# A chunked recurrence with a phase mixer on one core: each on-chip transpose either whole into one PSUM bank or as pairs of 64-row blocks into two, all eight banks in one tile, and a new table of the order

## The chip, the core and the metric

The kernel runs on one core of one Trainium2 chip. A core has a matrix engine (PE, with its weight loads shown apart as PEld), a vector engine (DVE), a scalar engine (ACT), GpSimd (POOL) and a queue engine (SP) that issues most DMAs. They run side by side and wait for each other through semaphores. PE writes to PSUM alone, which has eight banks; ACT and DVE copy from there to SBUF, and POOL works on SBUF.

The metric is the device time in microseconds. Before the change it is 198.57 us, the median of three runs (198.26 to 198.94). All inputs and the output are float32; the tolerance leaves room for bf16 matmuls, which both kernels use.

## What is computed

Two stages, the second on the output of the first. B = 4 batches, H = 8 heads, S = 768 tokens, D = 40.

```
state = zeros(B, H, D, D)
for t in range(S):
    y[:, :, t] = einsum('bhd,bhde->bhe', rt, state)
    Sa = einsum('bhde,bhe->bhd', state, at)
    state = state * wt[:, :, None, :] - einsum('bhd,bhe->bhde', Sa, bt)
    state = state + einsum('bhd,bhe->bhde', vt, kt)

x = y.transpose(0, 2, 1, 3).reshape(B, S, H * D)        # 4 x 768 x 320
theta = x @ w_theta
zr, zi = x * cos(theta), x * sin(theta)
u = x + einsum('ts,bsd->btd', w_tok_r, zr) + einsum('ts,bsd->btd', w_tok_i, zi)
out = u + maximum(u @ w_ch, 0)
```

## The kernel before

**Tiles.** The 768 tokens of a batch are cut into six chunks of 128; the 24 pairs of batch and chunk are the tiles i = 0 to 23, and a batch is six tiles in a row. In a tile the recurrence over 128 tokens becomes triangular products between matrices, two heads (64 padded rows each) side by side in a group of 128; there are four groups.

**Work of one tile**, by the names that the prediction uses:

- SP loads six arrays of 160 KB: w, k, b, a, v and r (`loads`; L409, and L421 for r and the first eight v).
- ACT takes the logarithm of w; PE makes its running sums (`cs`, L461); ACT makes the exponentials `ex` and `we`.
- POOL multiplies k and b by `ex` (`kb`, L429) and a by `we` (`ah`, L429).
- PE transposes these operands by matmuls against an identity: `tkb` (eight blocks of 128 by 128), `ta` (four), for tiles 8 and on `tv` (four), all at L391; for r and the first eight v `tr` and `to` (eight blocks for two tiles, L538) and `tb` (four, L557). ACT (L394) or DVE (L397) copies the result from PSUM to SBUF (`ekb`, `ea`, `ev`, `er`, `eb`).
- PE makes four score matrices: `spsi`, `sphi`, `slv`, `slu`, each by eight matmuls of 64 rows (L569). The two heads of a group use the upper and the lower 64 rows of the array, and write to two different banks. Each matrix of 128 by 1024 is masked on its way out by DVE (L578), or copied by ACT (L580) and masked by a select on POOL (L582).
- The chain from tile to tile: `x0` (L610, L616), copy `nx`, `nu` (L629), copy `enu`, then the new state `gt` (L652, L663, L667) and its copy for the readout `gd`; `nu` is transposed as well (`nut`, four blocks, L391).
- Readout: `y` (L793 to L802), times `we` on DVE, gives x.

**Work of the mixer.** For each two tiles, x is transposed (`xt`, five blocks, L711) and multiplied by w_theta (`th`, L763, L773). For each batch ACT makes sines and cosines, POOL the products `z` (L865), and for each of six output rows PE adds up twelve matmuls of 128 by 320 (`row`, L881). DVE adds x; then `ut` (five blocks, L711), `ch` (L763, L773), the last DVE operation and the store. The tokens' weights are transposed once (`wt`, six blocks each, L968).

**What sets the order.** Nothing is scheduled at run time or by a compiler: the code records 1602 operations (`Plan.add`), each with what it reads and writes, and then emits them in the order of the table `ORDER`. An engine runs its own operations in that order and waits at each for what it needs. `PICK` lists operations that run on their second engine instead of the first (a copy on DVE instead of ACT, for example). `HOMES` gives each PSUM result its bank. `WARM` puts matmuls on a constant in front of some early operations.

**PSUM before.** There are two tiles of two banks (`ps_d`) and four tiles of one bank (`ps_s`). The scores, which need two banks, go to the first; all else, transposes included, goes to the second, one bank each. A transpose of n blocks is n matmuls in the array's full 128-row mode.

## Time and profile before

The profile is one execution by the hardware profiler. Its own time is the span from its first to its last instruction.

| what | value |
|---|---|
| time, median of 3 runs | 198.57 us (198.26 to 198.94) |
| span of the profiled execution | 197.811 us |
| granted TensorE clock, mean | 1.000 |
| POOL: busy us, share | 145.1, 73% |
| moved by DMA | 32.75 MB, mean 166 GB/s |
| instructions of PE (matmuls) and PEld (weight loads) | 3288 each |

How to read it: a busy time is the union of an engine's instructions. Matmuls are pipelined, each is shown with its whole latency (some 0.2 to 0.3 us), and the next starts long before the one ahead has ended; so how dense PE runs is read from the distance between starts, in the timeline, and not from the busy time. A row of the timeline has the start in us, the length from the first start to the last end, the engine, the line, the operation, its shape, and the number of instructions that were merged. A row of the groups has the count after x, then the busy us and the mean ns of one, then the idle time ahead of them. The shape 64*128 means that 64 of the array's 128 rows are used.

### The profile page before, as it was taken

To read this page: it belongs to the slowest core of one execution; us is meant where nothing else is said; L and a number is where in the kernel's file an instruction comes from. 1 tells how busy PE (TensorE), PEld (TensorE's weight loads), DVE (VectorE), ACT (ScalarE), POOL (GpSimd) and SP (SyncE) were. 2 spreads that over 40 slices of the span, in tenths; PEclk is the share of its full clock that TensorE was granted. 3 is DMA by queue.
4 is the path that set the end of the run, shared out by engine and by line. 5 is a ranking of instruction groups with operands and counts; after the bars stand their busy time and mean duration, and the time that the engine had idled before them with its cause. 6 is when DMAs were issued, how large, how long until landed. Compare 5 with 4: busy or idle time off the path is not lost.

```text
span 197.8 us, 8019 instructions
## 1 busy us (share of the span) xinstructions
PE 187.6 (95%) x3288; PEld 150.3 (76%) x3288; DVE 164.3 (83%) x261; ACT 151.7 (77%) x337; POOL 145.1 (73%) x210
## 2 busy tenths in 40 slices
PE   7888999999989999999999999999999999999992
PEld 6776787777768788878878888888887878767661
DVE  5269899999989999888887988999999988675453
ACT  3584979799889988979988598888998986575111
POOL 8267544679879999699799939769699697558100
PEclk9999999999999999999999999999999999999999
DMA  6999879989999999999998899988998274863055
GB/s 119 210 212 163 154 161 196 182 166 197 233 174 173 207 171 185 190 185 223 153 210 168 153 187 170 188 148 169 182 155 163 43 177 102 87 194 104 0 191 174
DMA packets 134644, 32.75 MB, mean 166 GB/s; under 512 B 124816, under 2 KB 134608, under 8 KB 134608
## 3 DMA queue, kind: packets, MB, share of 16 engines
q1 hardware_dynamic: 131680, 29.19, 75.1%
q0 software_dynamic: 2784, 2.97, 9.6%
q8 instruction: 25, 0.41, 0.9%
q10 hardware_dynamic: 144, 0.08, 0.1%
q14 instruction: 11, 0.09, 0.1%
HBM read 29.54 MB, written 3.93 MB: 169 GB/s over the span
## 4 chain that ended last, share of the span: by engine, by line
PE 68%; DMA 9%; ACT 8%; SPq 6%; DVE 3%; issue 3%; POOL 1%; ACTq 0%; DVEq 0%; POOLq 0%
PE ps_s L881 17%; PE ps_s L391 10%; PE ps_d L569 9%; PE ps_s L763 5%; SPq L409 4%; DMA raw_w<-in_w_dram 3%; DMA raw_kb<-in_k_dram 3%; PE ps_s L711 3%; PE ps_s L652 2%; PE ps_s L629 2%; SPq L421 2%; DMA raw_r<-in_r_dram 2%; PE ps_s L538 2%; PE ps_s L773 2%; ACT cs L850 2%
## 5 line engine op out<-in xcount | busy, mean ns | idle before, releaser
L429 POOL TENSOR_TENSOR kb<-raw_kb,ex 128x320 bf16<-128x320 f32 x46 | 36.8, 811 | 9.7 <-DMA raw_kb<-in_k_dram 3.3
L881 PE MATMUL ps_s<-zr,wtok_r 128*128 128x320 bf16 x132 | 37.6, 299 | 0.0
L881 PE MATMUL ps_s<-zi,wtok_i 128*128 128x320 bf16 x132 | 37.5, 299 | 0.0
L578 DVE TENSOR_TENSOR lamu<-ps_d,mask_p 128x1024 bf16<-128x1024 f32 x22 | 26.8, 1219 | 1.7 <-PE ps_d L569 1.6
L578 DVE TENSOR_TENSOR psi<-ps_d,mask_p 128x1024 bf16<-128x1024 f32 x22 | 26.8, 1218 | 1.6 <-PE ps_d L569 1.4
L578 DVE TENSOR_TENSOR lamv<-ps_d,mask_p 128x1024 bf16<-128x1024 f32 x17 | 20.7, 1218 | 2.6 <-PE ps_d L569 1.8
L429 POOL TENSOR_TENSOR ah<-raw_a,we 128x320 bf16<-128x320 f32 x22 | 19.0, 866 | 3.6 <-DMA raw_a<-in_a_dram 1.6
L578 DVE TENSOR_TENSOR phi<-ps_d,mask_n 128x1024 bf16<-128x1024 f32 x17 | 20.7, 1218 | 0.9 <-PE ps_d L569 0.8
L865 POOL TENSOR_TENSOR zi<-cs,xp 128x320 bf16<-128x320 f32 x21 | 16.9, 816 | 3.3 <-ACT cs L850 3.3
L881 PEld LDWEIGHTS <-wtok_r 128*128 128x128 bf16 x144 | 14.0, 97 | 4.5
L569 PE MATMUL ps_d<-aT,kbT 64*128 64x128 bf16 x384 | 17.1, 217 | 0.2
L881 PEld LDWEIGHTS <-wtok_i 128*128 128x128 bf16 x144 | 14.1, 98 | 3.5
L391 PE MATMUL ps_s<-wide,kb 128*128 128x128 bf16 x184 | 15.0, 223 | 1.0 <-POOL kb L429 0.7
L865 POOL TENSOR_TENSOR zr<-cs,xp 128x320 bf16<-128x320 f32 x19 | 15.3, 810 | 0.7 <-ACT cs L850 0.7
L667 POOL TENSOR_TENSOR gt<-sum,ex 128x320 bf16<-128x320 f32 x13 | 9.5, 733 | 8.0 <-DVE sum L663 4.8
L800 PE MATMUL ps_s<-kb,lamv 128*128 128x40 bf16 x192 | 15.0, 180 | 0.0
L802 PE MATMUL ps_s<-kb,lamu 128*128 128x40 bf16 x192 | 14.9, 179 | 0.0
L569 PEld LDWEIGHTS <-kbT 64*128 64x128 bf16 x384 | 11.8, 94 | 3.1 <-ACT kbT L394 1.0
L800 PEld LDWEIGHTS <-lamv 128*128 128x128 bf16 x192 | 13.2, 96 | 0.6
L887 DVE TENSOR_TENSOR up<-ps_s,xp 128x320 bf16<-128x320 f32 x22 | 10.7, 488 | 3.5 <-PE ps_s L881 3.1
L435 POOL CAST r<-raw_r 128x640 bf16<-128x640 f32 x12 | 8.6, 720 | 6.5 <-DMA raw_r<-in_r_dram 6.5
L445 ACT ACTIVATE lw<-raw_w 128x320 bf16<-128x320 f32 x24 | 11.4, 475 | 2.6 <-DMA raw_w<-in_w_dram 2.6
(176 smaller groups left out, 606.7 us busy)
## 6 DMA issues: line engine op xcount, KB each, us to landing
raw_w<-in_w_dram SPq DMA_DIRECT2D x24, 160.0 KB, 4.1
raw_v<-in_v_dram SPq DMA_DIRECT2D x24, 160.0 KB, 3.9
raw_a<-in_a_dram SPq DMA_DIRECT2D x24, 160.0 KB, 4.2
raw_kb<-in_k_dram SPq DMA_DIRECT2D x24, 160.0 KB, 3.7
raw_kb<-in_b_dram SPq DMA_DIRECT2D x24, 160.0 KB, 4.0
raw_r<-in_r_dram SPq DMA_DIRECT2D x24, 160.0 KB, 4.4
out_dram<-oo SPq DMA_DIRECT2D x9, 160.0 KB, 2.0
wrow_i<-in_moe_w_tok_i_dram POOLq DMA_DIRECT2D x6, 192.0 KB, 5.3
```

Source lines behind the costliest of these rows:

```text
L391: nc.tensor.transpose(out=dst[:, c:c + 128], in_=pair(src, g), identity=ident)
L429: pool = ("POOL", lambda: nc.gpsimd.tensor_tensor(out=dst, in0=in0, in1=in1, op=ALU.mult))
L445: add("ACT", "ln", i, lambda: nc.scalar.activation(out=paired(lw)[:, :, :, 0:D], in_=paired(raw_w[s4]), func=AF.Ln), 473, [("raw_w", s4)], ...
L569: nc.tensor.matmul(t[:, q, g, :], lhsT=lhs[g][rows(q)], rhs=rhs[g][rows(q)], start=True, stop=True)
L578: add("DVE", kindm, i, lambda: nc.vector.tensor_tensor(out=flat, in0=whole(), in1=mask.to_broadcast([128, 2 * G, 128]), op=ALU.mult), 1217 ...
L667: add("POOL", "wgt", i, lambda: nc.gpsimd.tensor_tensor(out=new_state, in0=sum_t, in1=wm.to_broadcast([128, 8, D]), op=ALU.mult), 830, [(" ...
L763: nc.tensor.matmul(ps(pk)[:, 0:DM], lhsT=lhs[:, 3 * c + kt, :], rhs=wt[:, 3 * c + kt, :], start=kt == 0, stop=kt == 2, skip_group_check=n ...
L800: nc.tensor.matmul(o, lhsT=lamv[:, p, g, :], rhs=kb[:, 0, h, 0:D], start=first, stop=False, skip_group_check=True)
L802: nc.tensor.matmul(o, lhsT=lamu[:, p, g, :], rhs=kb[:, 1, h, 0:D], start=False, stop=True, skip_group_check=True)
L865: pool = ("POOL", lambda: nc.gpsimd.tensor_tensor(out=dst, in0=in0, in1=in1, op=ALU.mult))
L881: nc.tensor.matmul(acc(), lhsT=wtok[nm][j][:, s], rhs=zs[c][:, s], start=n == 0 and c == 0, stop=n == NT - 1 and c == 1)
L887: add("DVE", "uadd", q, lambda: nc.vector.tensor_tensor(out=u, in0=acc(), in1=x, op=ALU.add), 488, [pk, x_key(q)], [u_key(q)], at="row")
```

## The change

It has four parts.

1. The eight banks are one tile, `banks`; a result of two banks may lie in any two neighbouring ones.
2. A transpose may be whole as before (`new=(key, 1)`), or split: each block of 128 by 128 becomes two matmuls of 64 rows against a 64 by 64 identity, of which the one writes the first half of the result's columns to one bank and the other the second half to the next (`turned`, and `go` in `turn_runs`). The copy out of PSUM (`evac`) then reads both banks in one instruction, with one more level in its access pattern.
3. `PICK` now also says which transposes are split: 46 operations with 252 blocks in all: 72 of `tkb`, 40 each of `nut` and `tr`, 23 of `ut`, 18 of `wt`, 16 each of `ta` and `tb`, 11 of `xt`, 8 each of `tv` and `to`. Some operations change their engine: ACT goes from 327 to 310, DVE from 236 to 252, POOL from 185 to 189.
4. `ORDER`, `HOMES` and the place of the warm-up matmuls are new.

The diff, with the tables cut to a row each:

```diff
 ORDER = [
-    0, 7, 3, 6, 1, 2, 20, 8, 21, 23, 24, 4, 27, 9, 32, 30, 5, 22, 31, 33, 12, 25, 26, 34, 11,
...
-PICK = [
-    25, 31, 37, 39, 40, 48, 49, 75, 80, 85, 86, 115, 118, 130, 172, 180, 193, 203, 204, 222,
...
-WARM = {21: 25, 30: 4, 33: 1, 28: 8, 41: 11}
+PICK = {
+    26: 1, 32: 1, 36: 1, 38: 1, 40: 1, 41: 1, 48: 1, 49: 1, 75: 1, 77: 1, 78: 1, 85: 1, 86: 1,
...
+WARM = {21: (1, 25), 30: (0, 4), 33: (2, 1), 28: (6, 8), 41: (6, 11)}
...
-        for n in PICK:
-            self.ops[n].eng, self.ops[n].fn = self.ops[n].alts[0]
+        for n, m in PICK.items():
+            o = self.ops[n]
+            o.eng, o.fn = o.alts[m - 1][:2]
+            if o.eng == "PE":
+                o.new = (o.new[0], 2)
...
-    doubles = [psum.tile([128, 2, 512], FP32, name=f"ps_d{i}") for i in range(DOUBLE // 2)]
-    singles = [psum.tile([128, 512], FP32, name=f"ps_s{i}") for i in range(BANKS - DOUBLE)]
+    banks = psum.tile([128, BANKS, 512], FP32, name="banks")
...
-        return doubles[h[0] // 2] if len(h) == 2 else singles[h[0] - DOUBLE]
+        return banks[:, h[0]:h[0] + 2] if len(h) == 2 else banks[:, h[0]]
...
-    def transpose_pairs(dst, srcs):
-        for j, src in enumerate(srcs):
-            for g in range(G):
-                c = (j * G + g) * 128
-                nc.tensor.transpose(out=dst[:, c:c + 128], in_=pair(src, g), identity=ident)
...
-        act = ("ACT", lambda: copy_words(dst, ps(psk)[:, at]))
-        dve = ("DVE", lambda: copy_halves(dst, ps(psk)[:, at]))
+    def turned(kind, i, key, srcs, reads, cost, at="tile"):
+
+        def go():
+            if not split(key):
+                t = ps(key).bitcast(BF16)
+                for m, src in enumerate(srcs()):
+                    nc.tensor.transpose(out=t[:, m * 128:m * 128 + 128], in_=src, identity=ident)
+                return
+            for m, src in enumerate(srcs()):
+                for c in range(2):
+                    nc.tensor.transpose(out=ps(key)[:, c].bitcast(BF16)[:, m * 64:m * 64 + 64],
+                                        in_=src[rows(c)], identity=ident[rows(c), rows(c)])
...
+    def evac(eng, kind, i, psk, dst, n, writes=(), part=None):
+
+        def copy(op, out, dt, w):
+            one, src = n * w // 64, ps(psk) if w == 32 else ps(psk).bitcast(BF16)
+            if not split(psk):
+                at = (part or 0) * one
+                op(out=out, in_=src[:, at:at + one])
+            elif part is not None:
+                op(out=out, in_=src[:, part, 0:one])
+            else:
+                op(out=out.rearrange("p (n c w) -> p c n w", c=2, w=w),
+                   in_=src[:, :, 0:one // 2].rearrange("p c (n w) -> p c n w", w=w))
...
+            def words(x=x, dst=dst):
+                out = dst.bitcast(FP32)
+                if split(pr):
+                    nc.scalar.copy(out=out, in_=ps(pr)[:, x, 0:256])
+                    return
...
-                nc.tensor.matmul(t[:, 0:128], lhsT=busy[:, 0:128], rhs=busy[:, 0:128],
+            at, n = WARM[o.idx]
+            for _ in range(n):
+                nc.tensor.matmul(banks[:, at, 0:128], lhsT=busy[:, 0:128], rhs=busy[:, 0:128],
```

Three places show how the table moves instructions. In the rows, `banks` is the new tile for PSUM, and the number behind a name is the buffer's.

PE in tile 14, between `x0` and `nu`; `up_219` is a pair of mixer rows that `ut` transposes, `vT_195` and `kbT_188` are the weights of the scores `slv` and `sphi`. Before:

```order
L616 LDWEIGHTS psi_198
L616 MATMUL ps_s_253<-v_134,psi_198 128x40
L711 LDWEIGHTS up_219
L711 MATMUL ps_s_254<-wide,up_219 128x128
...
L569 LDWEIGHTS vT_195
L569 MATMUL ps_d_251<-rT_191,vT_195 128x128
```

The same place after the change:

```order
L606 LDWEIGHTS kbT_188
L606 MATMUL banks<-aT_185,kbT_188 128x128
L411 LDWEIGHTS up_219
L411 MATMUL banks<-wide,up_219 128x64
...
L666 LDWEIGHTS phi_200
L666 MATMUL banks<-nx_206,phi_200 128x40
```

The transpose of `up` has gone from the full mode ahead of the scores to ten matmuls of 64 rows and 64 columns behind them, in the mode that the scores have already set.

SP at the start of the program: the loads in the order of their issue. Before:

```order
L409 DMA raw_w_64<-in_w_dram 128x8x40
L421 DMA raw_v_77<-in_v_dram 128x1x320
L409 DMA raw_a_68<-in_a_dram 128x8x40
L421 DMA raw_v_77<-in_v_dram 128x1x320
L409 DMA raw_kb_73<-in_k_dram 128x8x40
L409 DMA raw_kb_73<-in_b_dram 128x8x40
L409 DMA raw_w_65<-in_w_dram 128x8x40
```

After:

```order
L439 DMA raw_w_64<-in_w_dram 128x8x40
L439 DMA raw_w_66<-in_w_dram 128x8x40
L439 DMA raw_w_65<-in_w_dram 128x8x40
L451 DMA raw_v_77<-in_v_dram 128x1x320
L439 DMA raw_kb_73<-in_k_dram 128x8x40
L451 DMA raw_v_77<-in_v_dram 128x1x320
L439 DMA raw_kb_73<-in_b_dram 128x8x40
L439 DMA raw_a_68<-in_a_dram 128x8x40
```

The w of tiles 1 and 2 is now loaded ahead of the other arrays of tile 0, whose last one, a, goes from the third place to the eighth.

POOL between the products of tile 4 (`kb_128`) and those of tile 5 (`kb_129`); AFFINE_SELECT is the mask of a score matrix that ACT has copied. Before:

```order
L429 TENSOR_TENSOR kb_128<-raw_kb_73,ex_174 128x8x40 x2
L435 CAST r_136<-raw_r_80 128x16x40
L429 TENSOR_TENSOR ah_127<-raw_a_68,we_179 128x8x40
L582 AFFINE_SELECT lamv_203<-lamv_203 128x1024
L429 TENSOR_TENSOR kb_129<-raw_kb_74,ex_175 128x8x40 x2
```

After:

```order
L459 TENSOR_TENSOR kb_128<-raw_kb_73,ex_174 128x8x40
L459 TENSOR_TENSOR ah_126<-raw_a_72,we_178 128x8x40
L619 AFFINE_SELECT lamv_203<-lamv_203 128x1024
L619 AFFINE_SELECT phi_201<-phi_201 128x1024
L465 CAST r_136<-raw_r_80 128x16x40
L459 TENSOR_TENSOR kb_129<-raw_kb_74,ex_175 128x8x40
L459 TENSOR_TENSOR ah_127<-raw_a_68,we_179 128x8x40
L992 DMA wrow_i_249<-in_moe_w_tok_i_dram 128x768
L619 AFFINE_SELECT psi_198<-psi_198 128x1024
L619 AFFINE_SELECT lamu_205<-lamu_205 128x1024
L459 TENSOR_TENSOR kb_129<-raw_kb_74,ex_175 128x8x40
```

Where one select stood there are four.

80 lines of the change are left out of this document (32 added, 48 removed), and 238 rows, old and new, of tables (HOMES, ORDER, PICK).

## The prediction

> **What bounds the kernel now.** I read three stretches of the windows first, then the chain of waits, then the timeline. In the rows of the windows the columns are the stretch, its length, then busy us (and instructions) of PE, PEld, DVE, ACT and POOL, then the granted clock, the DMA share and GB/s.
>
> ```profile
> span 197.8 us, 8019 instructions
> 0.00:60.00 60.00, 54.13 (x993) 44.14 (x993) 49.43 (x85) 46.29 (x112) 40.72 (x72) 1.00 0.94 181
> 60.00:160.00 100.00, 99.46 (x1871) 81.80 (x1870) 91.53 (x134) 88.71 (x195) 87.23 (x121) 1.00 0.94 171
> 160.00:197.80 37.80, 34.03 (x431) 24.39 (x428) 23.32 (x44) 16.68 (x32) 17.13 (x20) 1.00 0.50 127
> 57.00:80.00 23.00, 23.00 (x449) 18.96 (x445) 22.29 (x30) 21.64 (x53) 22.55 (x34) 1.00 1.09 185
> 80.00:120.00 40.00, 39.77 (x698) 32.24 (x696) 33.89 (x53) 34.17 (x74) 33.92 (x46) 1.00 0.97 181
> ```
>
> From 60 us on PE is never without work (99.46 of 100 us), while DVE (91.53), ACT and POOL have 8 to 13 us each to spare. Ahead of 60 us every engine has gaps. The chain of waits says why:
>
> ```profile
> 13.29 5.87 DMA raw_kb<-in_k_dram
> 30.21 4.23 DMA raw_r<-in_r_dram
> 48.11 6.82 DMA raw_w<-in_w_dram
> 55.73 0.44 PE ps_s L711 x5
> ```
>
> Three times the chain stands on a load (columns: start, us, what), the last until 54.9 us; behind that it is mostly PE. So the first 55 us are paced by loads that come at 181 GB/s, 0.9 us for 160 KB, and what PE saves there is worth little. What PE saves later is worth its full price, as long as DVE, at 91.5%, can follow.
>
> Now PE itself, from the distance between starts. Whole transposes and scores, at 83 us:
>
> ```profile
> 83.20 0.40 PE L569 MATMUL ps_d<-aT,kbT 64*128 64x128 bf16 x8
> 83.43 0.39 PE L569 MATMUL ps_d<-rT,nuT 64*128 64x128 bf16 x8
> 83.76 0.62 PE L391 MATMUL ps_s<-wide,kb 128*128 128x128 bf16 x8
> 84.22 0.30 PE L881 MATMUL ps_s<-zr,wtok_r 128*128 128x320 bf16 x1
> ```
>
> Eight whole blocks take 84.22 - 83.76 = 0.46 us, 0.056 a block (the rows are rounded to 0.01). Eight score matmuls of 64 rows take 83.43 - 83.20 = 0.23: four pairs at 0.056, so the two of a pair run side by side, and a pair costs what one whole matmul of 128 columns costs. The second eight end their issue at 83.43 + 0.23 = 83.66, and the transpose starts at 83.76: **a change of mode costs 0.10**. Once more:
>
> ```profile
> 108.60 0.71 PE L763 MATMUL ps_s<-wch,uT 128*128 128x320 bf16 x4
> 109.23 0.31 PE L773 MATMUL ps_s<-wch,uT 64*128 64x320 bf16 x2
> 109.38 0.61 PE L569 MATMUL ps_d<-aT,kbT 64*128 64x128 bf16 x16
> 109.92 0.31 PE L881 MATMUL ps_s<-zr,wtok_r 128*128 128x320 bf16 x1
> 110.07 0.30 PE L881 MATMUL ps_s<-zi,wtok_i 128*128 128x320 bf16 x1
> 110.21 0.30 PE L881 MATMUL ps_s<-zr,wtok_r 128*128 128x320 bf16 x1
> ```
>
> One whole matmul of 320 columns costs 0.14 (110.07 to 110.21); the pair of 320 costs 0.15 (109.23 to 109.38). Four whole ones from 108.60 end at 109.14, and the mode changes until 109.23: 0.09. Eight pairs from 109.38 end at 109.83, next start 109.92: 0.09 again. I take 0.095.
>
> **The split blocks.** A split block is a pair of 64 columns, which the trace does not show. Small matmuls do:
>
> ```profile
> 110.92 0.18 PE L800 MATMUL ps_s<-kb,lamv 128*128 128x40 bf16 x1
> 110.95 0.18 PE L802 MATMUL ps_s<-kb,lamu 128*128 128x40 bf16 x1
> 110.97 0.18 PE L800 MATMUL ps_s<-kb,lamv 128*128 128x40 bf16 x1
> 111.00 0.18 PE L802 MATMUL ps_s<-kb,lamu 128*128 128x40 bf16 x1
> ```
>
> Forty columns cost 0.025. Low end: the pair costs no more than that, 0.025. High end: each of its two matmuls costs it, 0.050. By columns, between 0.025 (40) and 0.056 (128), one matmul of 64 is about 0.030. I take 0.031, since both pairs above cost what one matmul of their columns costs. Saved: 0.056 - 0.031 = 0.025 a block (0.006 to 0.031). The change splits 252 blocks; of the operations that they belong to, 99 blocks ran before 60 us and 153 later. Later: 153 x 0.025 = **3.8 us** (0.9 to 4.7). Earlier: 2.5, taken as nothing.
>
> A rule speaks against this. The Trainium skill, TensorE: Matmul & The Clock Gate, Part 1, holds that the distance from start to start never falls below about 25 ns, however few the columns. By it a pair is 50 ns and the 153 blocks save 0.9; the pair in the first fence, at 56 ns for two, would fit either reading.
>
> **The changes of mode.** PE changes between full and 64-row mode 134 times before and 100 times after, as the order has it. By the time at which the operations ran before: 49 become 21 ahead of 60 us, 15 become 7 from 60 to 80, and 70 stay 70 behind (two more fall among the warm-up matmuls). At 0.095 that is 0.8 us from 60 us on, and 2.7 ahead of it, where the loads pace. The place in tile 14 shows the common case late in the program:
>
> ```profile
> 114.05 0.45 PE L711 MATMUL ps_s<-wide,up 128*128 128x128 bf16 x5
> 114.43 0.41 PE L569 MATMUL ps_d<-rT,vT 64*128 64x128 bf16 x8
> ```
>
> Five blocks (0.28) and a change of mode (0.10) before the scores; after the change the blocks follow the scores at 0.16, and the change of mode comes behind them instead.
>
> **The copies.** Masks, small copies and products change their engine. The prices:
>
> ```profile
> L578 DVE TENSOR_TENSOR psi<-ps_d,mask_p 128x1024 bf16<-128x1024 f32 x22 | 26.8, 1218 | 1.6 <-PE ps_d L569 1.4
> L397 DVE COPY kbT<-ps_s 128x1024 bf16<-128x1024 bf16 x8 | 5.5, 686 | 0.3 <-PE ps_s L391 0.2
> L397 DVE COPY aT<-ps_s 128x512 bf16<-128x512 bf16 x8 | 3.4, 420 | 0.8 <-PE ps_s L391 0.7
> L623 DVE CAST nx<-ps_s 128x320 bf16<-128x320 f32 x2 | 1.0, 486 | 0.2 <-PE ps_s L616 0.2
> L582 POOL TENSOR_SCALAR_AFFINE_SELECT phi<-phi 128x1024 bf16<-128x1024 bf16 x7 | 7.6, 1093 | 1.0 <-ACT phi L580 1.0
> L429 POOL TENSOR_TENSOR ah<-raw_a,we 128x320 bf16<-128x320 f32 x22 | 19.0, 866 | 3.6 <-DMA raw_a<-in_a_dram 1.6
> L435 POOL CAST r<-raw_r 128x640 bf16<-128x640 f32 x12 | 8.6, 720 | 6.5 <-DMA raw_r<-in_r_dram 6.5
> L865 POOL TENSOR_TENSOR zi<-cs,xp 128x320 bf16<-128x320 f32 x21 | 16.9, 816 | 3.3 <-ACT cs L850 3.3
> L546 ACT COPY rT<-ps_s 128x256 f32<-128x256 f32 x24 | 8.2, 378 | 1.6 <-DVE sx L482 0.8 <-PE ps_s L538 0.7
> L394 ACT COPY vT<-ps_s 128x256 f32<-128x256 f32 x21 | 7.6, 371 | 2.3 <-PE ps_s L391 1.2 <-PE ps_s L538 0.8
> ```
>
> DVE gives up three masks (-3 x 1.22), and takes 17 copies of 320 columns (`nx`, `enu`, `gd`, `th`; +17 x 0.48); the rest (transposed copies, three `z` fewer, one `ah` more) comes to about -0.9. In all **+3.7 us** on DVE. ACT loses some 4.3. POOL gets three selects more and three `z` more, +3.3 + 2.4, and a few casts less: +3.9. DVE and POOL have this time in the middle stretch, but DVE only just: its 91.5 us become some 94 in a stretch that is to shrink to 95 or 96, so some of its masks come late, and the scores' banks are free later. I give back 1.2 us for it (nothing to 3.7).
>
> Ten copies on DVE and 30 on ACT read two banks. The nearest row is `rT`, which reads two pieces at 378 ns against 371 for `vT` in one: 0.2 us in all on ACT, which has room. For DVE the far end is that such a copy falls from the rate of `kbT` to that of a mask, 1218 - 686 = 0.53 for 1024 elements; over its ten copies (some 7,600 elements) 3.9 us. I take it as nothing: each piece stays 64 neighbouring elements. A gain is excluded, since no element is left out.
>
> **Banks and waits.** One tile for all banks could make an access to one bank wait for another. The order says no: PE waits for DVE, ACT and POOL 524 times in both kernels, each time for the bank or the operand in question. So I take nothing.
>
> **The start.** The w of tiles 1 and 2 passes the loads of tile 0, so tile 0's last array comes two places later, 2 x 0.9 = 1.8 us. The whole set of tile 2 is complete at the same place in the queue as before, and the tiles behind it within one or two places. So the lag is gone by 20 us. I take nothing; the whole early stretch is open from -2 (its 5.2 us of saved PE time, in part on the chain) to +2.
>
> **Sum.** -3.8 - 0.8 + 1.2 = -3.4 us on the span of 197.8: 194.4. The runs' median of 198.57 lies 0.8 above that span, so the time predicted is **195.2 us**.
>
> **The rivals.**
>
> A. *DVE becomes the bound* and takes more than I gave. For it: 57:80, where all of DVE, PE and POOL are at 97% or more. If DVE cannot be denser than there (22.29 of 23.00, 96.9%), the 100 us with 91.5 + 2.6 to 3.7 of DVE work cannot be shorter than 97.1 to 98.3. Then 60 to 160 us gives 1.7 to 2.9 back instead of 4, and the rest some 0.5: **196.4**. Against it: from 80 to 120 us DVE has 6 us free (33.89 of 40).
>
> B. *Each half costs a full start.* At 0.050 a pair the blocks save 0.9, the modes 0.8, and DVE, less pressed, gives back 0.3: -1.4, **197.2**. For it: no row goes below 0.025. Against it: in the scores two matmuls cost what one does.
>
> C. *Slower: POOL starves tile 10.* Ahead of the products of tile 10 POOL has four selects more, one `o` and one `ah` more and one `r` less: 4 x 1.09 + 0.72 + 0.87 - 0.72 = 5.3 us. From 57 us on POOL is full (22.55 of 23.00). If the selects wait for their masks on ACT and so cannot use POOL's 19 us of idle time ahead of 60 us, the products of tiles 8 to 10, the state and the `z` are up to 5.3 late, and PE has no other work then: the mixer's rows hang on `z`. At the full price -3.4 + 5.3 = +1.9, **200.5**. It decides from 3.4 us on. Against it: the selects belong to tiles 1 to 4, early enough.
>
> D. *Slower: the copies of two banks* lose their rate on DVE: 3.9 more on 94.1 to 95.2 us in that stretch, over 0.969, is 101 to 102.3, less the 0.5 of the rest: **199.8** in the middle. It decides from 2.3 us on, 0.31 more for a copy of 1024.
>
> That the blocks are not run in pairs, or that the banks wait for each other, is excluded by the scores and the waits above, but for 2 in 100.
>
> **How the numbers follow.** My forecast 0.48, A 0.18, B 0.10, C 0.15, D 0.07, other 0.02. Forecast, A and B lie between 194 and 197.5; C and D at 199.8 and 200.5. The forecast's own range, from its prices at both ends, is 192.5 to 197; with the early stretch at its best 191. To leave out no more than 2 in 10 the range goes to 200.4. A change of 0.3% (0.6 us) is about what a measurement can tell here. Faster by more: nearly all of the forecast, most of A and B, 0.69. Within: 0.08, from A, B and C's mild end. Slower: C, D and the other, 0.23.
>
> **What would show it.** Right: a group of split blocks that starts every 0.03 us a pair; 100 changes of mode; PE still above 99% from 60 us on, with the end earlier by the saving. Wrong: pairs at 0.05 (B); DVE at 97% with PE gaps that end on DVE (A); PE waiting for POOL's kb between 55 and 85 us (C); copies of two banks on DVE near 1.2 us (D). A saving early that reaches the end would show as loads landing sooner, and would make my zero for the first stretch wrong.

## The result and the profile after

The changed kernel takes 205.91 us, median of three runs (204.93 to 205.94), against 198.57 before: a ratio of 1.036, 95% interval 1.032 to 1.040. It is slower. The prediction was 195.2 us, faster, with a range that ended at 200.4; it is wrong in sign. Times here and below are medians over all executions of a version; the ratios leave out executions in a slower state of the chip, and each profile is of one execution, up to 2.6 us beside its version's median.

The profiled execution has a span of 204.2 us, 6.4 more than before. The windows first, the three stretches that the prediction opened with and six shorter ones; the columns are those of the prediction (busy us and instructions of PE, PEld, DVE, ACT, POOL, then granted clock, DMA share, GB/s). After:

```profile
span 204.2 us, 8518 instructions
0.00:60.00 60.00, 46.49 (x902) 39.22 (x903) 39.11 (x76) 39.10 (x89) 37.67 (x66) 0.97 0.97 182
60.00:160.00 100.00, 98.63 (x2082) 80.83 (x2080) 94.75 (x149) 88.84 (x193) 91.75 (x124) 1.00 0.92 168
160.00:204.20 44.20, 39.65 (x565) 29.10 (x562) 32.07 (x54) 20.38 (x41) 19.71 (x26) 0.99 0.55 115
0.00:10.00 10.00, 4.88 (x43) 4.12 (x44) 2.81 (x25) 3.29 (x7) 5.38 (x26) 1.00 0.87 176
50.00:60.00 10.00, 6.73 (x111) 5.34 (x108) 6.80 (x8) 6.11 (x13) 4.41 (x7) 0.83 0.96 177
60.00:80.00 20.00, 19.03 (x395) 16.16 (x393) 19.60 (x29) 19.30 (x42) 18.76 (x27) 1.00 0.98 171
```

The same short stretches before:

```profile
0.00:10.00 10.00, 7.90 (x69) 6.82 (x70) 4.28 (x28) 4.59 (x9) 5.44 (x26) 1.00 0.84 165
50.00:60.00 10.00, 8.80 (x186) 7.22 (x182) 8.88 (x11) 8.65 (x23) 8.13 (x11) 1.00 1.06 201
60.00:80.00 20.00, 20.00 (x397) 16.54 (x396) 19.36 (x27) 18.64 (x44) 19.55 (x30) 1.00 1.10 186
```

In the first 60 us every engine does less than before (DVE 39.11 against 49.43 us), with more instructions left for the end (160 us to the end: 565 matmuls against 431). Two stretches stand out: the first 10 us, and 50 to 60 us, where all engines are slack at once and the granted clock is 0.83.

To see where the time went, I follow one operation of the chain from tile to tile: the start of the first `x0` matmul (before L616, now L653; the last rows of the two fences on the start, below, are tile 0's). Cut at four of the 24 tiles, each number the us between two such starts:

| profiled execution | start to tile 3 | 3 to 10 | 10 to 12 | 12 to 23 | tile 23 to the end | span |
|---|---|---|---|---|---|---|
| before | 31.1 | 48.3 | 13.3 | 77.9 | 27.2 | 197.8 |
| after | 39.2 | 48.9 | 13.7 | 74.3 | 28.1 | 204.2 |
| difference | +8.1 | +0.6 | +0.4 | -3.6 | +0.9 | +6.4 |

So a late saving came: 3.6 us in tiles 12 to 23, of which 2.3 are left from tile 10 to the end, where 3.4 had been forecast from 60 us on. It is outweighed by 8.1 us that are lost ahead of tile 3 and never made up; 7.7 of them are there already at tile 0 (20.16 against 12.43 us). How far two executions can differ here shows in e2 below, which has the old order: 1.1 us in tiles 3 to 10, 0.1 elsewhere.

A second sum, over PE alone. From the distance between successive matmul starts I take each one's own cost as the dense rows show it and 0.092 us for a change of mode; what is left is lost time, that is, waits and what matmuls at half speed cost on top.

| PE, us | before | after |
|---|---|---|
| until the first matmul starts | 1.1 | 4.1 |
| own cost of all matmuls | 163.5 | 157.4 |
| changes of mode (134, 100) | 12.3 | 9.2 |
| lost time | 17.1 | 29.5 |
| of it ahead of 20 us, 20 to 60, 60 to 100, behind | 7.3, 5.8, 1.3, 2.7 | 9.4, 13.2, 3.9, 3.0 |

PE's work shrank by 6.1 and its mode changes by 3.1, as the prediction had it (6.3 and 3.5). Against that PE lost 12.4 us more than before and started 2.9 later.

**The start.** PE, ACT and one mask on DVE in the timeline after (start, length, engine, line, operation, count, and the idle time ahead with what ended it):

```profile
3.53 0.47 ACT L475 ACTIVATE lw<-raw_w 128x320 bf16<-128x320 f32 x1 [1.44 <-DMA raw_w<-in_w_dram]
4.05 0.43 PE L506 MATMUL banks<-lw,mask_p 128*128 128x320 bf16 x1 [4.05 <-ACT lw L475]
4.26 2.87 PE L1041 MATMUL banks<-busy 128*128 128x128 bf16 x25
6.93 0.48 PE L491 MATMUL banks<-lw,ntri_inc 128*128 128x328 bf16 x1
...
7.59 0.83 ACT L475 ACTIVATE lw<-raw_w 128x320 bf16<-128x320 f32 x2 [3.59 <-PE banks L494]
...
16.11 1.23 DVE L615 TENSOR_TENSOR psi<-banks,mask_p 128x1024 bf16<-128x1024 f32 x1 [4.51 <-PE banks L606]
...
18.27 0.65 ACT L587 COPY rT<-banks 128x256 f32<-128x256 f32 x2 [2.62 <-PE banks L575]
18.81 1.04 ACT L617 ACTIVATE phi<-banks 128x1024 bf16<-128x1024 f32 x1
...
19.72 0.39 ACT L429 COPY v<-banks 128x256 f32<-128x256 f32 x1
...
20.16 0.43 PE L653 MATMUL banks<-v,psi 128*128 128x40 bf16 x8
```

And PE and that mask before:

```profile
1.13 2.85 PE L1019 MATMUL ps_s<-busy 128*128 128x128 bf16 x25 [1.13 <-DVE busy L268]
4.02 0.43 PE L461 MATMUL ps_s<-lw,ntri_inc 128*128 128x328 bf16 x1
...
11.15 1.23 DVE L578 TENSOR_TENSOR psi<-ps_d,mask_p 128x1024 bf16<-128x1024 f32 x1 [0.52 <-PE ps_d L569]
...
12.43 0.37 PE L616 MATMUL ps_s<-v,psi 128*128 128x40 bf16 x8
```

The 25 warm-up matmuls need no load. Before, they filled PE's wait for the first w. In the new order another running sum of tile 0 (L506) stands ahead of them, so PE waits 4.05 us for ACT's first logarithm, and only then runs the 2.7 us of warm-ups, with the sum that ACT and all products wait for (`cs`, L491) behind them: 6.93 instead of 4.02. ACT's next logarithms need a buffer that this sum frees, and wait 3.59. Of the 7.7 us at tile 0, 5.0 are there when its mask `psi` starts (16.11 against 11.15). The rest comes behind it: before, `x0` starts when that mask ends; now it starts 2.8 us later than that, since it also waits for a copy of v, which ACT makes at 19.72, behind two copies of r that wait 2.62 for PE and behind ACT's copy of another score matrix.

**The stand-still at 50 us.** DVE and PE after:

```profile
49.80 1.23 DVE L615 TENSOR_TENSOR phi<-banks,mask_n 128x1024 bf16<-128x1024 f32 x1
50.94 1.22 DVE L615 TENSOR_TENSOR lamu<-banks,mask_p 128x1024 bf16<-128x1024 f32 x1
52.07 0.41 DVE L427 COPY vT<-banks 128x512 bf16<-128x512 bf16 x1
```

```profile
50.07 0.21 PE L653 MATMUL banks<-v,psi 128*128 128x40 bf16 x2
52.54 0.30 PE L716 MATMUL banks<-wide,gt 128*128 128x80 bf16 x4 [2.27 <-DVE vT L427]
...
53.46 1.02 PE L407 MATMUL banks<-wide,kb 128*128 128x128 bf16 x8
```

A transpose of v for two tiles (`to`) is split now, so it holds two banks until both its copies are done. One copy was moved from ACT to DVE, where it stands behind two masks of 1.2 us. PE's next operation (`gd` of tile 4) has the second bank as its home and waits 2.4 us from start to start. Behind it the same eight whole blocks take 53.46 to 54.28, 0.10 each instead of 0.056: the matmuls run at half speed for some 3 us.

### The profile page after: what moved, and what is told of

It reads as the page before. It is cut to its first block, busy times and chain, and to the rows that moved or that the text cites. A ratio compares the mean times of both kernels' runs of the same rounds, so it can differ in the third digit from the quotient of the medians.

```text
span 204.2 us, 8518 instructions
## 1 busy us (share of the span) xinstructions
PE 184.8 (90%) x3540; PEld 149.1 (73%) x3540; DVE 165.9 (81%) x277; ACT 148.3 (73%) x320; POOL 149.1 (73%) x214
## 4 chain that ended last, share of the span: by engine, by line
PE 57%; DVE 8%; DMA 5%; ACT 3%; issue 1%; SPq 1%; DVEq 0%; ACTq 0%
PE banks L913 17%; PE banks L407 9%; PE banks L606 7%; PE banks L795 6%; DMA wch<-in_moe_w_ch_dram 3%; DVE psi L615 2%; DMA vT<-v 2%; PE banks L805 2%; PE banks L411 2%; PE banks L666 2%; PE banks L689 2%; DVE lamu L615 1%; PE banks L653 1%; PE banks L834 1%; PE banks L647 1%
## 5 line engine op out<-in xcount | busy, mean ns | idle before, releaser
L913 PE MATMUL banks<-zr,wtok_r 128*128 128x320 bf16 x144 | 40.8, 300 | 0.0
L913 PE MATMUL banks<-zi,wtok_i 128*128 128x320 bf16 x144 | 40.7, 299 | 0.0
L615 DVE TENSOR_TENSOR psi<-banks,mask_p 128x1024 bf16<-128x1024 f32 x21 | 25.6, 1219 | 5.5 <-PE banks L606 4.5
L615 DVE TENSOR_TENSOR lamu<-banks,mask_p 128x1024 bf16<-128x1024 f32 x23 | 28.0, 1219 | 1.1 <-PE banks L606 1.0
L615 DVE TENSOR_TENSOR lamv<-banks,mask_p 128x1024 bf16<-128x1024 f32 x18 | 21.8, 1218 | 3.1 <-PE banks L606 3.0
L606 PE MATMUL banks<-aT,kbT 64*128 64x128 bf16 x384 | 18.0, 222 | 2.1 <-ACT aT L425 0.7
L615 DVE TENSOR_TENSOR phi<-banks,mask_n 128x1024 bf16<-128x1024 f32 x13 | 15.8, 1217 | 0.2
L832 PE MATMUL banks<-kb,lamv 128*128 128x40 bf16 x192 | 15.0, 180 | 0.0
L834 PE MATMUL banks<-kb,lamu 128*128 128x40 bf16 x192 | 14.9, 179 | 0.0
L832 PEld LDWEIGHTS <-lamv 128*128 128x128 bf16 x192 | 13.2, 96 | 1.0 <-issue 0.5
L834 PEld LDWEIGHTS <-lamu 128*128 128x128 bf16 x192 | 13.0, 96 | 0.0
```

The source lines that it names most:

```text
L606: nc.tensor.matmul(t[:, q, g, :], lhsT=lhs[g][rows(q)], rhs=rhs[g][rows(q)], start=True, stop=True)
L615: add("DVE", kindm, i, lambda: nc.vector.tensor_tensor(out=flat, in0=whole(), in1=mask.to_broadcast([128, 2 * G, 128]), op=ALU.mult), 1217 ...
L832: nc.tensor.matmul(o, lhsT=lamv[:, p, g, :], rhs=kb[:, 0, h, 0:D], start=first, stop=False, skip_group_check=True)
L834: nc.tensor.matmul(o, lhsT=lamu[:, p, g, :], rhs=kb[:, 1, h, 0:D], start=False, stop=True, skip_group_check=True)
L913: nc.tensor.matmul(acc(), lhsT=wtok[nm][j][:, s], rhs=zs[c][:, s], start=n == 0 and c == 0, stop=n == NT - 1 and c == 1)
```

## The experiments

After the result the theory was that the new matmuls are as cheap as forecast and that a few waits which the order makes eat the saving: the warm-ups at the start, the copy at 50 us. Its rivals were that the one tile for all banks or the two-bank copies cost time, that the splits are worth less than their PE time, and that the whole early order is at fault and no single place. Ratios are to the kernel before on the same chip, with the 95% interval; the changed kernel has 1.036. Tables of numbers are cut to a row.

### Which part holds the loss

**e2_old_tables**: the new code (one tile for the banks, the new transposes and copies) with the order, homes and engines of before, nothing split.

```diff
 ORDER = [
-    0, 20, 12, 23, 21, 119, 8, 69, 72, 120, 121, 22, 73, 24, 7, 1, 6, 2, 32, 3, 122, 70, 71, 25,
...
+    0, 7, 3, 6, 1, 2, 20, 8, 21, 23, 24, 4, 27, 9, 32, 30, 5, 22, 31, 33, 12, 25, 26, 34, 11,
...
```

> The changed kernel's code, with its single tile of banks, with the four tables of the kernel before: nothing split, the old order, homes and engines. If one tile makes no access wait for another bank's: 198.6 us, within 0.6. If it does (rival): more than 199.5 us, with TensorE gaps that the kernel before has not.

Measured 199.03 us, ratio 1.000 (0.997 to 1.003). The one tile costs nothing that shows (the interval is 0.6 us either way); the loss is in the tables, which also say what is split.

**e3_start_t2, e4_start_t6, f5_old_to_77**: the first 150, 360 and 612 operations in the order of before (with its homes and engines), the rest as after. The diff is of the same kind, over more rows each time.

> The first 150 of the 1602 operations stand in the order of the kernel before, with its engines and whole transposes (up to x0 of tile 2, 25 us); the rest is the changed kernel. Theory S (the start alone costs, 7.5 us of TensorE time lost by tile 2): 198 to 199 us, and less if the gap of 2.4 us at 50 us goes with it, 195 to 196. Rival (the loss is in the order of the whole early stretch): above 201 us.

> As the run with 150, but the first 360 operations as before (up to x0 of tile 6, 50 us). Theory S: x0 of tile 6 at 50 us, the late saving as predicted (3.4 us less than the kernel before): 195 to 196 us. If the late part is no better than before's and only catches up because it was late: 198 us or more.

> The first 612 operations as before (to 77 us, x0 of tile 9), the rest as changed. Theory P (the late term of the sum holds: some 135 blocks at 0.025 less, and the changes of mode): 195.5 to 197 us, 1.5 to 3 less than the kernel before. Rival (the late order gives back what the blocks save, in waits for DVE and DMA): 198 us or more.

Measured: 208.75 us, 1.048 (1.041 to 1.054); 203.27, 1.019 (1.014 to 1.023); 206.37, 1.030 (1.020 to 1.040). By the cut of the table above:

| | to tile 3 | 3 to 10 | 10 to 12 | 12 to 23 | behind | span |
|---|---|---|---|---|---|---|
| e2 | 31.0 | 47.2 | 13.3 | 77.8 | 27.2 | 196.5 |
| e3 | 37.0 | 48.9 | 15.1 | 74.4 | 29.7 | 205.1 |
| e4 | 32.5 | 50.3 | 14.3 | 73.7 | 29.3 | 200.1 |
| f5 | 30.6 | 48.6 | 19.9 | 73.7 | 29.3 | 202.1 |

With an old beginning the old times come back as far as it reaches, and the late stretch saves 3.5 to 4.2 in all three. But each loses at its seam. e3 has tile 2 at 24.7 as before and then waits (ACT once for 1.7 us for a w), since the rows behind count on loads that the old start issues later. f5 stands once for 3.8 us: PE's waits in 60 to 100 us (what is waited for, us in total, times, longest):

```profile
PE banks L403 <- ACT lamv L613: 3.8, 1, 3.8
```

An order is a whole; a part of one put ahead of a part of another makes waits of its own. So these runs show that the loss lies early and the gain late, but not what a clean early order would give.

### The waits that were named

**e1_warm_first**: the warm-ups ahead of the running sum that waits.

```diff
-WARM = {21: (1, 25), 30: (0, 4), 33: (2, 1), 28: (6, 8), 41: (6, 11)}
+WARM = {23: (1, 25), 30: (0, 4), 33: (2, 1), 28: (6, 8), 41: (6, 11)}
```

> One edit to the changed kernel: the 25 warm-up matmuls stand ahead of cx of tile 0 instead of ahead of its cs, so they no longer wait for the first lw. Theory W (a good part of the late start is that these matmuls stand behind a wait): TensorE begins near 1.1 us instead of 4.05, cs of tile 0 near 4.4 instead of 6.9, x0 of tile 0 2.5 to 3 us sooner, and the end follows by as much: 202.9 to 203.5 us. Theory L (the loads and the work of tiles 1 and 2 put ahead of tile 0 set the start, whatever the warm-ups do): x0 of tile 0 moves by less than 1 us, 205 to 206 us.

Measured 205.87 us, 1.030 (1.024 to 1.037). Tile 0 comes 2.1 us sooner, tiles 3 and 10 only 1.1 and 1.0, and the end not at all by its profile (span 204.7): near the end PE now waits for a transposed x that a DMA brings.

**f1_eo_act**: the copy at 50 us back on ACT, behind the other copy of the same two banks; operation 364 leaves the list of second engines too.

```diff
-    116, 361, 362, 338, 355, 333, 354, 501, 313, 314, 315, 316, 339, 364, 340, 500, 363, 178,
+    116, 361, 362, 338, 355, 333, 354, 501, 313, 314, 315, 316, 339, 340, 500, 363, 364, 178,
...
-    348: 1, 359: 1, 362: 1, 364: 1, 366: 1, 391: 1, 407: 1, 409: 1, 410: 1, 442: 1, 464: 1, 507:
+    348: 1, 359: 1, 362: 1, 366: 1, 391: 1, 407: 1, 409: 1, 410: 1, 442: 1, 464: 1, 507: 1, 525:
```

> One operation of the changed kernel moves: eo of tile 7, the copy of the second half of the split transpose to 6, goes from DVE, where it stands behind two masks (1.23 + 1.22 us), to ACT, straight behind the copy of the first half. Theory B (this copy holds bank 7, gd of tile 4 wants that bank, and TensorE stands 2.4 us): the gap at 50 us goes, and the cold matmuls behind it; x0 of tile 6 comes 2 to 3 us sooner and the end with it, 203 to 204 us. Rival (DVE paces the stretch from 48 to 80 us and the gap is only where it shows): the gap moves to the next wait for DVE, x0 of tile 10 gains less than 0.7 us, 205.3 to 206 us.

Measured 205.64 us, 1.030 (1.021 to 1.040). At the place itself it does all that was expected. PE in its timeline, with no wait:

```profile
48.79 0.30 PE L716 MATMUL banks<-wide,gt 128*128 128x80 bf16 x4
...
49.92 0.61 PE L407 MATMUL banks<-wide,kb 128*128 128x128 bf16 x8
```

The eight blocks run at full speed. From `x0` of tile 5 to that of tile 8 it takes 16.9 us instead of 20.3: 3.4 gained. But in this profile it is lost again at 156 us; two of f1's four executions took only 204.4 and 204.3 us, and whether the same happens in them is not known. DVE and POOL there, and PE behind them:

```profile
155.72 0.44 POOL L465 CAST v<-raw_v 128x320 bf16<-128x320 f32 x1
155.89 3.29 DVE L458 TENSOR_TENSOR ah<-raw_a,we 128x320 bf16<-128x320 f32 x1
156.13 0.78 POOL L897 TENSOR_TENSOR zi<-cs,xp 128x320 bf16<-128x320 f32 x1
...
156.88 0.80 POOL L459 TENSOR_TENSOR kb<-raw_kb,ex 128x320 bf16<-128x320 f32 x1
157.63 0.45 POOL L465 CAST v<-raw_v 128x320 bf16<-128x320 f32 x1
158.04 0.80 POOL L459 TENSOR_TENSOR kb<-raw_kb,ex 128x320 bf16<-128x320 f32 x1
...
159.64 0.30 PE L716 MATMUL banks<-wide,gt 128*128 128x80 bf16 x4 [2.57 <-DVE xp L841]
```

The product `ah` of tile 22, which the change moved from POOL to DVE, takes 3.29 us, and PE stands for 2.6 us at the end of it; from 160 to 170 us the granted clock is 0.84. In the profile of the changed kernel the same product takes 0.62, beside one POOL product that takes longer than its usual 0.8:

```profile
160.22 0.62 DVE L458 TENSOR_TENSOR ah<-raw_a,we 128x320 bf16<-128x320 f32 x1
160.44 1.05 POOL L897 TENSOR_TENSOR zi<-cs,xp 128x320 bf16<-128x320 f32 x1
```

**g2_eo_ah**: f1 with that product back on POOL; 1414 leaves the list.

```diff
-    1279: 1, 1306: 1, 1324: 1, 1328: 1, 1399: 1, 1400: 1, 1414: 1, 1421: 1, 1422: 1, 1429: 1,
+    1306: 1, 1324: 1, 1328: 1, 1399: 1, 1400: 1, 1421: 1, 1422: 1, 1429: 1, 1430: 1, 1437: 1,
```

> As the run with the copy of tile 7 on ACT, and ah of tile 22 back on POOL, where the kernel before has it. In three runs this product took 2.8 to 3.3 us on DVE instead of 0.62, while POOL ran products and casts without a break, and the gain of the moved copy was lost there. Theory P (a DVE product of two SBUF operands is shut out by POOL's): no DVE instruction of that place takes over 1.3 us, the gap of 2.7 us at 157 us is gone, 202.5 to 203.5 us (ratio 1.017 to 1.022). Rival (DVE is behind there for another reason): the gap stays in another form, 205 us.

Measured 204.10 us, 1.021 (1.013 to 1.029): the long product is gone, and PE waits 1.7 us for POOL to do it instead.

**h1_three**: all three repairs, the edits of e1, f1 and g2.

> The changed kernel with three small repairs and nothing else: the 25 warm-ups first, the copy of tile 7 on ACT, ah of tile 22 on POOL. From the single runs: 2 us at tile 0 of which about 1 was left at tile 10, 3.2 us at tile 10 from the copy, and no product of 3 us on DVE. If they add up: x0 of tile 10 at 83 to 84 us, 200.5 to 202.5 us, ratio 1.007 to 1.018. If each only uncovers the next wait (rival): 203.5 us or more.

Measured 202.66 us, 1.022 (1.015 to 1.028); span 200.2. That is just beyond the 200.5 to 202.5 (1.007 to 1.018) of repairs that add up in full, and short of the rival's 203.5.

**i1_ah_early**: h1 with that product some places earlier on POOL.

```diff
-    1397, 1411, 1330, 1329, 1179, 1181, 1182, 854, 1337, 1402, 1375, 1187, 1183, 872, 1352,
-    1403, 1353, 1359, 1472, 873, 1376, 1415, 1377, 1416, 1417, 1404, 874, 1378, 1414, 1360,
+    1397, 1411, 1414, 1330, 1329, 1179, 1181, 1182, 854, 1337, 1402, 1375, 1187, 1183, 872,
+    1352, 1403, 1353, 1359, 1472, 873, 1376, 1415, 1377, 1416, 1417, 1404, 874, 1378, 1360,
```

> As the run with three repairs, and ah of tile 22 stands 2.5 us earlier on POOL, ahead of a cast, a z and a product. There TensorE waited 1.9 us for it. If that wait is what was left behind 100 us: the gap at 155 us goes, 200 to 201.3 us, ratio 1.007 to 1.015. If another wait takes its place: 202 us or more.

Measured 203.57 us, 1.023 (1.015 to 1.031); span 200.6. PE's longest waits behind 60 us, of h1 and of i1:

```profile
PE banks L407 <- POOL ah L459: 1.7, 1, 1.7
```

```profile
PE banks L795 <- DMA xT<-xp: 1.7, 1, 1.7
```

One wait goes, another comes, and the total stays. By tiles:

| | to tile 3 | 3 to 10 | 10 to 12 | 12 to 23 | behind | span |
|---|---|---|---|---|---|---|
| before | 31.1 | 48.3 | 13.3 | 77.9 | 27.2 | 197.8 |
| after | 39.2 | 48.9 | 13.7 | 74.3 | 28.1 | 204.2 |
| e1 | 38.1 | 49.0 | 14.1 | 73.7 | 29.8 | 204.7 |
| f1 | 37.8 | 45.5 | 14.2 | 77.7 | 30.0 | 205.2 |
| h1 | 36.0 | 45.4 | 14.3 | 75.6 | 28.9 | 200.2 |
| i1 | 36.9 | 45.4 | 14.3 | 73.6 | 30.4 | 200.6 |

With the stand-still at 50 us mended, tiles 3 to 10 run 2.9 us faster than before the change (1.8 faster than in e2); with the wait at 155 us gone, tiles 12 to 23 run 4.3 faster. What keeps these versions slower than before is the 5 to 6 us ahead of tile 3, 1 us at tiles 10 to 12, and 1.7 to 3.2 at the end.

**h3_keep_warm**: the changed kernel with 32 matmuls on a constant in the stand-still at 50 us. They compute nothing that is used.

```diff
-WARM = {21: (1, 25), 30: (0, 4), 33: (2, 1), 28: (6, 8), 41: (6, 11)}
+WARM = {21: (1, 25), 30: (0, 4), 33: (2, 1), 28: (6, 8), 41: (6, 11), 334: (1, 32)}
```

> The changed kernel with 32 more warm-up matmuls in the gap of 2.4 us at 50 us, into a bank that is free there; the gap stays as long. If the granted clock falls because TensorE stands still (six transposes at 0.107 us behind the gap): no matmul behind the gap is slow, and x0 of tile 8 comes 0.8 to 1.5 us sooner against x0 of tile 5 than in the changed kernel (20.3 us there). If the clock falls for another reason: the same 20.3 us.

Measured 204.28 us, 1.026 (1.019 to 1.034). PE in its timeline:

```profile
49.64 1.95 PE L1041 MATMUL banks<-busy 128*128 128x128 bf16 x32
52.06 0.30 PE L716 MATMUL banks<-wide,gt 128*128 128x80 bf16 x4 [0.47 <-DVE vT L427]
...
52.90 0.61 PE L407 MATMUL banks<-wide,kb 128*128 128x128 bf16 x8
```

The wait for DVE is still there, but the blocks behind it run at full speed (0.61 instead of 1.02). Tile 5 to tile 8 takes 18.9 us: of the 3.4 us that f1 gained there, 1.4 are the half speed and, by subtraction, 2.0 the wait.

### What the splits are worth

**f6_whole_late**: the changed kernel with its 24 splits behind tile 11 (125 blocks) whole again, which also adds eight changes of mode. They leave the list; the order stays. One row of it:

```diff
-    1279: 1, 1306: 1, 1324: 1, 1328: 1, 1399: 1, 1400: 1, 1414: 1, 1421: 1, 1422: 1, 1429: 1,
+    1145: 1, 1156: 1, 1157: 1, 1159: 1, 1160: 1, 1167: 1, 1276: 1, 1306: 1, 1324: 1, 1399: 1,
```

> The changed kernel with the 24 late splits undone: 125 blocks that run behind x0 of tile 11 (94 us) are whole again, at the same places and with the same homes; 8 more changes of mode. If TensorE's time counts in full late: 125 x 0.0265 + 8 x 0.095 = 4.1 us more, 209.5 to 210.5 us. If another engine paces the late part: under 1.5 us more.

Measured 210.66 us, 1.055 (1.046 to 1.063): 11.5 us over the kernel before on its chip, where the changed kernel is 7.3 over, so 4.2 more (some 1.9 either way, by the two intervals). In PE's sum its own cost rises by 3.1 and the changes of mode by 0.7, and the lost time between 100 and 160 us stays at about 1 us. So in these profiles nothing hides the 3.8 us. The rest of the two spans does not compare as cleanly: f6 also has a long product `ah` at 161 us (2.83), and 2 us less lost ahead of 60.

**g4_split_in_place**: the old order, engines and start, with those 11 transposes (72 blocks) split for which two neighbouring banks are free at their old place, or three to eight places off.

```diff
-    25: 1, 31: 1, 37: 1, 39: 1, 40: 1, 48: 1, 49: 1, 75: 1, 80: 1, 85: 1, 86: 1, 115: 1, 118: 1,
+    25: 1, 31: 1, 37: 1, 39: 1, 40: 1, 48: 1, 49: 1, 75: 1, 77: 1, 80: 1, 85: 1, 86: 1, 115: 1,
+    118: 1, 127: 1, 130: 1, 172: 1, 180: 1, 182: 1, 193: 1, 203: 1, 204: 1, 222: 1, 230: 1, 233:
...
```

> The kernel before in the new code, with its order, engines and homes, but 11 transposes of 72 blocks split where two neighbouring banks are free and no change of mode is added; three of them move by 6 to 8 places on TensorE to stand beside scores. 72 x 0.0262 = 1.9 us of TensorE time less, 1.5 of it behind 60 us. If the late saving counts in full: 196.9 to 197.5 us, ratio 0.990 to 0.994, faster than both kernels. If the copies of two banks or the banks that are held longer give it back: 198.5 us or more.

Measured 201.02 us, 1.011 (1.008 to 1.013). PE's own work falls by 1.8 us, 0.025 a block, as priced; its lost time is 20.8, against 15.8 in e2 and 17.1 before, so 3.7 to 5.0 more. Two of its waits, of which e2 has the first at 1.0 and the second not:

```profile
PE banks L401 <- POOL ah L453: 2.4, 2, 1.4
PE banks L405 <- DVE phi L609: 1.1, 1, 1.1
```

The second is the price of the second bank: the split transpose waits for a mask on DVE that must first empty it. The other waits are not traced to a bank. So in the old order these splits gave back more than they saved, and only 72 of the 252 blocks came near a place with two free banks there.

### Whether the start can be mended

The last group looked for a beginning that keeps the late gain. **f4_start_set** and **g1_start_own** take the first 153 operations of the changed kernel, which are another set than those of before, and put them in the old relative order, in g1 with the loads in the changed kernel's order. **g3_start_eo_ah** is g1 with the repairs of g2. The first row of f4 becomes that of e2 above; that of g1:

```diff
-    0, 20, 12, 23, 21, 119, 8, 69, 72, 120, 121, 22, 73, 24, 7, 1, 6, 2, 32, 3, 122, 70, 71, 25,
+    0, 12, 8, 7, 1, 6, 2, 3, 4, 5, 9, 19, 18, 11, 10, 15, 14, 13, 16, 17, 20, 90, 53, 55, 54,
```

> The first 153 operations of the changed kernel (to x0 of tile 2), the same set, in the relative order of the kernel before, with its engines and whole transposes; all later rows as changed. Unlike the run with the old first 150, every load and every early w that the rest counts on is there. Theory S (the order of the start costs): x0 of tile 2 some 4 to 5 us sooner than in the changed kernel, and at least 3 of it left at tile 10 and at the end: 201 to 203 us. Rival (the stretch from 25 to 60 us has a pace of its own, set by ACT and DVE): the gain is gone by tile 8, 205 us or more.

> The same first 153 operations of the changed kernel, with SP's loads in the changed order, but the work of all other engines among them in the relative order of the kernel before, with its engines, whole transposes and the warm-ups at the very start. Unlike the two runs before, no load that the later rows count on comes later. Theory S (the order of PE and ACT at the start costs, not that of the loads): x0 of tile 2 at 25 to 26.5 us instead of 30.6, at least 3 us left at tile 10, and 201 to 203 us (ratio to the kernel before 1.010 to 1.022). Rival (the stretch from 25 to 60 us has a pace of its own): x0 of tile 3 at 37 us or later, as in the other runs, 205 us or more.

> The three repairs together: start, copy of tile 7, product of tile 22. If they add up: 198 to 200 us (ratio 0.995 to 1.005), which leaves the dense stretch from 60 to 100 us as the rest of the loss. If the early stretch has its own pace, the start repair adds nothing to the others: 202 us or more.

Measured: 209.96 us, 1.047 (1.034 to 1.060); 210.14, 1.051 (1.044 to 1.058); 206.73, 1.035 (1.028 to 1.042). f4 has tile 0 at 12.3, like before, and tile 3 at 40.2, later than the changed kernel. Its ACT waits for a load (20 to 60 us):

```profile
ACT lw L474 <- DMA raw_w<-in_w_dram: 4.4, 1, 4.4
```

**h2_early_14**, **h2_early_11** and **i2_early_ah** start from h1 and put its first operations, some 430 to 480, in orders of their own, loads included (with homes to match). First row of h2_early_14:

```diff
-    0, 20, 12, 23, 21, 119, 8, 69, 72, 120, 121, 22, 73, 24, 7, 1, 6, 2, 32, 3, 122, 70, 71, 25,
+    0, 8, 6, 20, 23, 69, 12, 24, 72, 21, 70, 7, 32, 71, 2, 1, 22, 119, 3, 4, 26, 116, 33, 122,
```

> The three repairs, and the first 430 of the 1602 operations moved by up to some dozens of places so that in ACT, DVE, POOL and TensorE no operation stands long behind one that waits (mphi and eb of tile 0 ahead of the er that wait for TensorE, and so on); engines and splits of the changed kernel stay, so do the rows behind x0 of tile 7. Theory O (the lost time is the order of the first 60 us on in-order queues; the splits themselves and the late order are good): x0 of tile 0 near 12.5, of tile 3 near 31, of tile 10 at 76 to 79 us, and 195.5 to 198 us, faster than both kernels (ratio 0.98 to 0.997). Rival E (the early stretch has a pace that no order mends, since the changed rows need the split copies and two banks each): x0 of tile 3 at 36 us or later, 200 us or more.

> The same kind of early order, found independently. Theory O: within 1 us of the run before. Rival E: 200 us or more.

> The same, with the first 480 operations, the loads among them, in an order that was found anew with the loads taken at the pace that the two orders before it were held to (0.92 to 1.02 us for 160 KB, the transfers of POOL's queue among them). Theory O (order, and loads that come when they are wanted): x0 of tile 3 at 30 to 33 us, of tile 12 at 91 to 95 us (92.7 in the kernel before, 95.7 with three repairs), 196 to 199 us, ratio 0.985 to 1.002. Rival E (what the early rows cost does not go away by order): tile 12 at 97 us or later, 201 us or more.

Measured: 209.59 us, 1.053 (1.048 to 1.059); 208.72, 1.048 (1.041 to 1.054); 207.56, 1.034 (1.028 to 1.040). All miss. They bring tile 0 forward (15.2 and 14.2 in the two h2) and then wait for loads; in h2_early_14, 10 to 62 us:

```profile
POOL o L465 <- DMA raw_v<-in_v_dram: 3.9, 1, 3.9
```

Its tile 3 stands at 35.8 like h1's (35.5 in h2_early_11), though its tile 0 comes 1.9 us sooner than h1's 17.1, and tile 10 stands at 88.1 like the changed kernel's. A better start was not found, and none of these kernels beats the one before.

## Why the prediction was wrong, step by step

**The split pair, right.** PE, behind the tile 14 that the prediction looked at:

```profile
120.74 0.40 PE L411 MATMUL banks<-wide,kb 64*128 64x64 bf16 x16
120.97 0.28 PE L411 MATMUL banks<-wide,ah 64*128 64x64 bf16 x8
```

Eight pairs in 0.23 us, 0.029 each, where 0.031 was taken. Rival B, 0.050 a pair, is false. So is, for pairs of 64 rows, the rule of the Trainium skill that was set against it (TensorE: Matmul & The Clock Gate, Part 1): the two matmuls of a pair in the first row start 3 to 4 ns apart. (A straight line between the prediction's prices for 40 and 128 columns gives 0.033 for 64, not the 0.030 that it names; the measured price lies below both.)

**Changes of mode, right.** 100, at 0.092 each.

**The late stretch, right in its prices, two thirds of the sum.** -3.4 us was the sum from 60 us on. Tiles 12 to 23 took 3.6 less, but from tile 10 to the end it is 2.3, and 60 to 80 us lost time too (below). f6 shows that the gain is the splits and their changes of mode: undone, 3.8 us of PE work come back. In i1, with its wait at 155 us removed, the stretch saves 4.3.

**Copies of two banks, and one tile for all banks: nothing, right.** On DVE a copy of 1024 elements from two banks (L429) and from one (L425), after:

```profile
L429 DVE COPY kbT<-banks 128x1024 bf16<-128x1024 bf16 x4 | 2.7, 686 | 0.1
L425 DVE COPY kbT<-banks 128x1024 bf16<-128x1024 bf16 x3 | 2.1, 685 | 0.2 <-PE banks L407 0.2
```

686 against 685 ns: rival D is false. e2 shows the tile neutral.

**"The start ... the lag is gone by 20 us. I take nothing": the step that failed most.** The lag at tile 3 is 8.1 us, and 7.7 of it stand at tile 0. I counted places in SP's queue of loads, and did so rightly: the last of tile 0's w, v, k, b and a lands at 9.16 us instead of 7.93, 1.2 later where 1.8 was counted. But in the changed kernel its k, b and a then lie for 1.6 to 3.1 us before they are used, and the arrays from tile 2 on mostly for 5 to 10. (In h1, where PE starts as early as before, tile 0's are used 0.1 to 0.5 us after they land, so there its loads are waited for again.) What waited was PE, behind a running sum put ahead of the warm-ups, and ACT behind PE. The range of "-2 to +2" for the whole early stretch was thus taken from the loads and from PE's saving alone, because loads paced it before.

Of the 8.1 us, the warm-ups' place is worth 1.1 to 1.8 (after and e1, 39.2 and 38.1; f1 and h1, 37.8 and 36.0). Another 1.4 to 2.1 is the speed of PE in the first 20 us, which differs between executions of one order: after and e1 stayed at half speed for longer (last section). Of the other 5, h1's lag at tile 3, 4.7 us stand at its tile 0, where the mask `psi` starts 2.9 later than before and `x0` waits 1.8 behind it for the same copy of v. So the place is known. The cause is not shown: no run moved that copy alone, and in the two h2, whose tile 0 comes 1.9 and 2.9 sooner than h1's, tile 3 gains 0.2 and 0.4. PE's lost time in h1 is 2.9 us above that of before in the first 20 us and 3.8 above it from 20 to 60, spread over many waits for ACT and DVE, and no new beginning brought tile 3 below 35.5. This stays open, as do the 1.7 to 3.2 us that the repaired versions lose behind tile 23.

**"Banks and waits ... I take nothing": failed.** That PE waits 524 times in both orders was true and said nothing of how long. A split result holds two banks, and both are free only after the last copy; `gd` of tile 4 waited 2.4 us for that, 2.0 of which were still missing at tile 8, and PE lost 1.4 more at half speed; f1 and h3 show both parts, 3.4 in all. The prediction had named POOL, DVE and ACT as suppliers, but priced no wait for a bank. g4 has one more such wait, of 1.1 us, where the old order is otherwise kept.

**The early saving "taken as nothing": not settled.** In h1 tiles 3 to 5 take 10.5 us, against 13.3 before and 12.7 in e2. So what PE saves there can reach the path; in the changed kernel the stand-still behind tile 5 eats it. But h1 is 4.9 us late at tile 3, so that its loads there lie ready some 1 to 5 us ahead of their use. Whether the saving would come with a start as early as before, where loads set the pace, no run shows.

**The give-back of 1.2 us for DVE: too small, in the place it named.** From 60 to 80 us DVE is busy for 19.60 of 20 us and ACT for 19.30, and PE, which had no gap there before, is at 19.03; its lost time in 60 to 100 us rises by 2.6. That is rival A's mechanism, with about twice my price, though DVE got denser (98%) than the 96.9% that A took for its limit. It is shown by the windows only: no run took copies off DVE there.

**Rival C, POOL starves tile 10: its condition came, its effect did not.** Waits over the whole program, after:

```profile
POOL phi L619 <- ACT phi L617: 7.3, 3, 6.8
...
POOL zr L897 <- ACT cs L882: 6.8, 5, 5.6
```

A select did wait for its matrix on ACT, as the rival had it, for 6.8 us until 19.92, and POOL's products behind it wait as well; later POOL stands 5.6 us for ACT's cosines. But from 55 to 85 us PE has no wait for POOL in the list. The products of tile 8 come 11.5 us later than before behind those cosines, and not because POOL is full: it is busy for 4.41 of the 10 us ahead of 60 us.

In short, the prediction priced each instruction well and the waits of the schedule hardly at all. It was held that a new order of 1602 operations costs nothing where no new kind of wait appears. The order's waits were the result.

## What to carry to other kernels

A change of order must be priced by its waits: for every operation that moves, ask what is now ahead of it on its engine and when that gets its input, the first microseconds most of all, where work that needs no input should stand ahead of work that does. A result that lies in two PSUM banks frees neither place early, so its copies should stand on engines that are free then, and its home should not be the next one that PE needs. And a wait of 2 to 3 us on PE costs more than its length, since the matmuls behind it may run at half speed; where it can't be removed, matmuls on a constant cover that part.
